# Two tiles at a time in the second half of MoE1, GpSimd subtractions in three slots, and gathers between index loads

## Chip, core and metric

One core of one Trainium2 chip runs the kernel. The metric is the device time of one execution in microseconds (us), as the median of several runs. Engines: TensorE (PE), VectorE (DVE), ScalarE (ACT), GpSimd (POOL) and SyncE (SP, which only issues DMAs).

## What is computed

```python
attn = pooled_attention(q, k, v)        # 8 batches x 8 heads x 576 x 64, k and v mean-pooled by 8
x = attn.transpose(0, 2, 1, 3).reshape(4608, 512)
x = (np.maximum(x @ w_in, 0) ** 2) @ w_out             # MoE1: 512 -> 2048 -> 512
logits = x @ w_gate                                    # MoE2: 8 experts, 512 -> 1024 -> 512
e = argmax(logits, axis=1); p = softmax(logits)[range(4608), e]
out[mask_e] = p[mask_e, None] * (np.maximum(x[mask_e] @ w1[e], 0) @ w2[e])
```

## The kernel before

Everything is fp32 carried through TensorE as pairs: a value is split into a high part (the value rounded to fp32r) and a low part (the rest, rounded), and each product is the sum of three, high·high, high·low and low·high. Tokens go in 18 tiles of 256 (NT); d_ff goes in chunks of 128.

**First half of MoE1** (chunks 0 to 7; names h_a, y_a) runs beside the attention. Each tile's split x is written to DRAM (xs_d), and so is its partial y (yp_d). **Second half** (chunks 8 to 15; names h_b, y_b) is 144 steps, 18 tiles by 8 chunks. A step is layer 1 of a chunk (`layer1`, L291: 12 matmuls of 256 columns into one PSUM tile h), the activation (`act_square_b`, L322 to L325: relu and two squares on ACT, the subtraction gl_b on DVE), some work from a queue, and layer 2 (`layer2`, L342: 6 matmuls of 512 columns) of the chunk two steps back (LAG). `load_xb` brings a tile's xh and xl back from xs_d.

**Routing.** After a tile's last chunk `route` adds the first half's y (L1017, DVE) and puts 16 logits (L1021, DVE: product and sum, written as junk and lg) and a chain of further steps into a queue: rank (L1040 to L1053, DVE), count (L1059, PE, tile pc), place (L1070 to L1087, DVE), two scatters of the positions to perm_d (L1092, POOL, the second waits for the landing of the first) and the store of y to y_d (L1097, POOL). `run_queue` is called twice in a step; the numbers of `many` say how many entries each call runs. After tile 13 (TA) a table of experts is made (table A), then `gather_index` loads each slot's index column (L1244, POOL, pidx) and `gather_rows` gathers its token rows by indirect DMA (L1251, POOL, xg).

**MoE2** (names h_s, y_s) goes in 17 slots of up to 256 tokens of one expert, 8 chunks each, with the same step. A chunk's weights are loaded six items ahead (raw_s, SP) and split three ahead: high part on ACT (L194, wh_s), low part on DVE (L195, wl_s). `slot_xT` transposes gathered rows on PE (L1266, px) and splits them (xh_s on ACT, xl_s on DVE, L610). `act_relu` (L331, L332) makes gh on ACT by a relu of h, and gl on DVE from h and gh; h comes free when both have read it. `moe2_finish` scales y (ACT for the first half of a slot, DVE, L1291, for the second) and scatters both to the output (L1292, POOL). From slot 6 on, half-filled slots are mixed in (hh, hy, hs). Each engine works its instructions off in the order in which the program issues them; the step functions, the queue and two tables of functions by step (`pre`, `post`) set that order:

```python
many = (2, 1) if g < N1 else (1, g % 2)
side = [lambda: run_queue(many[0])]
...
run_queue(many[1])
```

Of the kernel before, what the change touches and what calls it, by code (L numbers as in the profile page):

```python
# [45 lines left out]
def moe_pipeline_kernel(  # L46
# [236 lines left out]
    def layer1(w, x, nm):  # L283
        wh, wl = w
        xh, xl = x
        h = ps_h.tile([P, 256], F32, tag="h", name=f"h_{nm}")
# [6 lines left out]
        return h  # L293

    def act_square(h, nm):
        r = gpool.tile([P, 256], F32, tag="r", bufs=2, name=f"r_{nm}")
        g = gpool.tile([P, 256], F32, tag="g", bufs=2, name=f"g_{nm}")
        gh = gpool.tile([P, 256], F32R, tag="gh", name=f"gh_{nm}")
        gl = gpool.tile([P, 256], F32R, tag="gl", name=f"gl_{nm}")
# [85 lines left out]
    stream = Stream()  # L385

# [966 lines left out]
    def half_step(j, w, first=0, end=NHALF_MOST):  # L1353
        wh, wl = w
        if j < end * NCH:
# [8 lines left out]
            if kk == NK - 1:  # L1364
                hs = halves["pool"].tile([P, 512], F32, tag="hs", name=f"hs_{t}_{half}")
# [12 lines left out]
        if j >= first * NCH + HLAG:  # L1378
# [8 lines left out]
            if c == NCH - 1:  # L1387
                yo = gpool.tile([P, 512], F32, tag="yo", bufs=3, name=f"hyo_{t}")
# [24 lines left out]
    N1 = NT * NCH  # L1413
# [7 lines left out]


# [31 lines left out]
    for i in range(3):  # L1454
        put(pre, i, lambda i=i: wch_b.append(split_raw(fetched[NCH - 3 + i], f"f{NCH - 3 + i}")))
    put(pre, 3, begin_b)
    for ti in range(NT):
        if ti:
            put(pre, (ti - 1) * NCH + 2, lambda ti=ti: xb.update({ti: load_xb(ti)}))
        put(pre, ti * NCH + 4, lambda ti=ti: ypb.update({ti: load_yp(ti)}))  # L1460

    state = None
    for i_, (what, g) in enumerate(items):
# [10 lines left out]
        many = (2, 1) if g < N1 else (1, g % 2)  # L1474
        side = [lambda: run_queue(many[0])]
        if g < N1:
            x = xb[i]
            stream.step(wch_b[c], x, act_square_b, c, state, f"b{i}_{c}",
                        lambda ys, i=i: route(i, ys, ypb[i]), side)
        else:  # L1480
            s = i - NT
# [4 lines left out]
            stream.step(chunks.pop(g - N1), sx[s][0], act_relu, c, state, f"s{s}_{c}", moe2_finish(s), side)  # L1486
# [39 lines left out]
```

## Time and profile before

| | us |
|---|---|
| median of 3 runs (lowest, highest) | 1522.07 (1522.02, 1524.66) |
| the profiled execution | 1524.06 |
| its span, first to last instruction | 1522.5 |
| PE busy in the span | 1461.9 (96%) |
| DVE busy | 1112.9 (73%) |
| ACT busy | 658.2 (43%) |
| POOL busy | 410.2 (27%) |

A group of instructions is told by its line, its engine and what it writes and reads. Times of an instruction run from its start to its end; matmuls overlap, so what one costs is the distance from its start to the start of the next. "Idle before, releaser" says what an engine waited for. The second half of MoE1 runs from about 605 to 1016 us, the slots from there to the end.

### The profile page before, as it was taken

How to read it: one execution, taken by the hardware profiler on the slowest of the kernel's cores; microseconds unless marked ns; L12 is line 12 of the kernel's file. 1: busy time of each engine (PE TensorE's matmuls, PEld its weight loads, DVE VectorE, ACT ScalarE, POOL GpSimd, SP SyncE). 2: the span in 40 equal slices, each digit the busy share in tenths (PEclk: the TensorE clock that was granted, in tenths of full speed). 3: DMA queues.
4: the chain of work that ended last, by engine and by line, in shares of the span. 5: the costliest groups of instructions: out<-in, count | busy, mean ns of one | idle time of the engine just before them, and what ended most of it. 6: DMA issues, size and time to landing. Idle time of an engine off the chain costs nothing. (4 is left out here: it accounts for less than half of the span.)

```text
span 1522.5 us, 26605 instructions
## 1 busy us (share of the span) xinstructions
PE 1461.9 (96%) x9382; PEld 1317.4 (87%) x9382; DVE 1112.9 (73%) x2360; ACT 658.2 (43%) x1376; POOL 410.2 (27%) x507
## 2 busy tenths in 40 slices
PE   5789999999999999999999999999999999999997
PEld 4678889898989999999999999988889888888886
DVE  8986797689867554477777777778785777767763
ACT  4443333233333323433434334345544666655652
POOL 3253334344434444001111111131222222212101
PEclk8799999999999999999999999999999999999998
DMA  9225354456523214765677666578986888888862
GB/s 295 98 88 165 123 155 164 135 174 169 164 87 101 93 61 158 223 97 75 108 98 76 106 97 76 134 158 213 208 253 222 257 258 276 274 254 279 257 223 91
DMA packets 208617, 249.03 MB, mean 164 GB/s; under 512 B 56479, under 2 KB 134431, under 8 KB 208352
## 3 DMA queue, kind: packets, MB, share of 16 engines
q1 hardware_dynamic: 197408, 217.54, 52.1%
q0 software_dynamic: 11072, 29.75, 9.2%
q8 instruction: 75, 1.23, 0.4%
q14 instruction: 62, 0.51, 0.2%
HBM read 193.28 MB, written 55.28 MB: 163 GB/s over the span
## 5 line engine op out<-in xcount | busy, mean ns | idle before, releaser
L1021 DVE CUSTOM_DVE_ANT_0 junk<-yr,wgb 128x512 f32<-128x512 f32 x288 | 198.2, 688 | 4.7
L195 DVE TENSOR_TENSOR wl_s<-raw_s,wh_s 128x1024 fp32r<-128x1024 f32 x136 | 165.6, 1223 | 39.7 <-ACT wh_s L194 38.2
L194 ACT CAST wh_s<-raw_s 128x1024 fp32r<-128x1024 f32 x136 | 141.2, 1046 | 19.7 <-DMA raw_s<-in_moe_w_dram 19.6
L322 ACT ACTIVATE r_b<-h_b 128x256 f32<-128x256 f32 x144 | 55.4, 385 | 213.2 <-PE h_b L291 210.9
L300 ACT ACTIVATE r_a<-h_a 128x256 f32<-128x256 f32 x130 | 50.0, 384 | 212.3 <-PE h_a L291 146.7
L302 POOL TENSOR_TENSOR g_a<-r_a 128x256 f32<-128x256 f32 x130 | 84.3, 649 | 183.7 <-ACT r_a L300 183.2
L1092 POOL DMA_INDIRECT perm_d<-pos,di x36 | 38.7, 1076 | 348.0 <-DVE es L1083 163.2
L325 DVE TENSOR_TENSOR gl_b<-g_b,gh_b 128x256 fp32r<-128x256 f32 x144 | 61.3, 425 | 96.4 <-ACT g_b L324 96.4
L303 POOL TENSOR_TENSOR gl_a<-g_a,gh_a 128x256 fp32r<-128x256 f32 x130 | 97.6, 751 | 102.8 <-DVE gh_a L301 55.2
L342 PE MATMUL y_a<-wh_m,gh_a 128*128 128x512 f32 x288 | 120.4, 418 | 0.0
L342 PE MATMUL y_a<-wh_m,gl_a 128*128 128x512 f32 x288 | 114.8, 399 | 1.0 <-POOL gl_a L314 1.0
L342 PE MATMUL y_a<-wl_m,gh_a 128*128 128x512 f32 x288 | 115.3, 400 | 0.0
L342 PE MATMUL y_b<-wh_f,gh_b 128*128 128x512 f32 x288 | 113.8, 395 | 0.0
L342 PE MATMUL y_b<-wl_f,gh_b 128*128 128x512 f32 x288 | 113.6, 394 | 0.0
L342 PE MATMUL y_b<-wh_f,gl_b 128*128 128x512 f32 x288 | 112.0, 389 | 0.0
L1292 POOL DMA_INDIRECT out_dram<-yo,tidx x34 | 39.5, 1161 | 263.0 <-ACT yo L1289 167.0
L301 DVE SCALAR_TENSOR_TENSOR gh_a<-h_a,r_a 128x256 fp32r<-128x256 f32 x130 | 54.2, 420 | 76.3 <-ACT r_a L300 75.6
L342 PE MATMUL y_s<-wh_s,gh_s 128*128 128x512 f32 x272 | 107.3, 395 | 0.0
L342 PE MATMUL y_s<-wl_s,gh_s 128*128 128x512 f32 x272 | 107.2, 394 | 0.0
L342 PE MATMUL y_s<-wh_s,gl_s 128*128 128x512 f32 x272 | 106.1, 390 | 0.0
L331 ACT ACTIVATE gh_s<-h_s 128x256 fp32r<-128x256 f32 x136 | 52.4, 385 | 114.0 <-PE h_s L291 113.4
L291 PE MATMUL h_a<-xh,wh_m 128*128 128x256 f32 x576 | 98.1, 293 | 2.1 <-ACT r_a L311 1.5
(323 smaller groups left out, 3912.6 us busy)
## 6 DMA issues: line engine op xcount, KB each, us to landing
raw_s<-in_moe_w_dram SPq DMA_DIRECT2D x272, 256.0 KB, 4.2
raw_h<-in_moe_w_dram SPq DMA_DIRECT2D x112, 256.0 KB, 4.0
y_d<-yr POOLq DMA_DIRECT2D x18, 514.0 KB, 10.1
xs_d<-xh SPq DMA_DIRECT2D x18, 512.0 KB, 2.7
xs_d<-xl SPq DMA_DIRECT2D x18, 512.0 KB, 3.3
yp_d<-ya SPq DMA_DIRECT2D x36, 256.0 KB, 2.1
xh_b<-xs_d SPq DMA_DIRECT2D x18, 512.0 KB, 8.5
xl_b<-xs_d SPq DMA_DIRECT2D x18, 512.0 KB, 11.3
```

The lines of the kernel that those rows point to most:

```text
L194: nc.scalar.copy(wh, raw)
L195: nc.vector.tensor_tensor(wl, raw, wh.bitcast(F32), ALU.subtract)
L291: nc.tensor.matmul(h, w_[:, 0, kk * P:(kk + 1) * P], rhs[:, kk, :], start=n == 0, stop=n == 3 * NK - 1)
L300: nc.scalar.activation(r, h, AF.Relu)
L301: nc.vector.scalar_tensor_tensor(gh, h, 0.0, r, op0=ALU.max, op1=ALU.mult)
L302: nc.gpsimd.tensor_tensor(g, r, r, ALU.mult)
L303: nc.gpsimd.tensor_tensor(gl, g, gh.bitcast(F32), ALU.subtract)
L322: nc.scalar.activation(r, h, AF.Relu)
L325: nc.vector.tensor_tensor(gl, g, gh.bitcast(F32), ALU.subtract)
L331: nc.scalar.activation(gh, h, AF.Relu)
L342: nc.tensor.matmul(ys[u], lhs[:, ts], rhs[:, 1, :], start=(c == 0 and n == 0), stop=(c == NCH - 1 and n == 2))
L1021: nc.vector.tensor_tensor_reduce(out=junk, in0=yr[:, u, 0:DM], in1=wgb[:, e, :], scale=1.0, scalar=0.0, op0=ALU.mult, op1=ALU.add, accum_o ...
```

## The change

1. The second half of MoE1 goes in pairs of tiles: `pair_layer1` does a chunk for 512 tokens with 12 matmuls of 512 columns, `pair_act` the activation at that width, layer 2 is unchanged and done for one tile and then for the other, one step back and not two. N1 counts pairs, so there are 72 such steps; `load_pair` brings x in eight DMAs for a pair, in two sets of buffers.
2. In slots 0, 1 and 2 `act_relu_early` makes the relu of h twice on ACT (one fp32r, one fp32), and GpSimd subtracts the one from the other; from slot 3 on `act_relu` stands. The tiles of gh and gl, and those for the scaled y, come from one ring of eight (`ring`).
3. Queue entries in a slot step: (2, 1) in the first eight, (1, 1) up to the 24th, then as before. The table after tile 13 and the first six steps after tile 17 are put in the chain's free places.
4. `after_a` alternates gathers with index loads, and slot 0's rows are transposed in the last two steps of the pairs.

```diff
+    def pair_layer1(w, x, nm):
+        wh, wl = w
+        xh, xl = x
+        h = ps_h.tile([P, 512], F32, tag="h", name=f"h_{nm}")
+        n = 0
+        for w_, x_ in ((wh, xh), (wh, xl), (wl, xh)):
+            for kk in range(NK):
+                nc.tensor.matmul(h, w_[:, 0, kk * P:(kk + 1) * P], x_[kk // 2][:, kk % 2, :], start=n == 0, stop=n == 3 * NK - 1)
+                n += 1
+        return h
...
+    def pair_act(h, nm):
+        r = gpool.tile([P, 512], F32, tag="r", bufs=2, name=f"r_{nm}")
+        g = gpool.tile([P, 512], F32, tag="r", bufs=2, name=f"g_{nm}")
+        gh, gl = ring(f"gh_{nm}"), ring(f"gl_{nm}")
         nc.scalar.activation(r, h, AF.Relu)
         nc.scalar.activation(gh, r, AF.Square)
         nc.scalar.activation(g, r, AF.Square)
...
+    def act_relu_early(h, nm):
+        gh, gl = g_tiles(nm)
+        g = sq_tiles(nm)[0]
+        nc.scalar.activation(gh, h, AF.Relu)
+        nc.scalar.activation(g, h, AF.Relu)
+        nc.gpsimd.tensor_tensor(gl, g, gh.bitcast(F32), ALU.subtract)
         return gh, gl
...
         if ti == TA:
+            fs[10:14] = steps(table_a(), 4)
             fs += after_a()
         if ti == NT - 1:
-            fs += after_b()
+            more = after_b()
+            fs[10:16] = more[:6]
+            fs += more[6:]
...
     def after_a():
-        return (steps(table_a(), 4) + [None] * 2 + [lambda s=s: gather_index(s) for s in range(NSLOT_A)]
-                + [None] * 3 + [lambda s=s: gather_rows(s) for s in range(4)])
+        idx, rows = ([lambda s=s, f=f: f(s) for s in range(NSLOT_A)] for f in (gather_index, gather_rows))
+        return [idx[0], idx[1], None, None, rows[0], idx[2], rows[1], idx[3], rows[2], idx[4], rows[3], idx[5]]
...
-    N1 = NT * NCH
+    N1 = NT // 2 * NCH
...
-        many = (2, 1) if g < N1 else (1, g % 2)
+        many = (2, 1) if g < N1 else (2, 1) if g < N1 + 8 else (1, 1) if g < N1 + 24 else (1, g % 2)
...
-            stream.step(chunks.pop(g - N1), sx[s][0], act_relu, c, state, f"s{s}_{c}", moe2_finish(s), side)
+            stream.step(chunks.pop(g - N1), sx[s][0], act_relu_early if s < 3 else act_relu, c, state, f"s{s}_{c}", moe2_finish(s), side)
```

How the order of instructions moves is shown at three places. PE in the second half of MoE1, before: layer 2 of one chunk and layer 1 of another (x4: four matmuls in a row):

```order
L291 MATMUL h_b_4_8262<-xh_b_7871,wh_f_6926 128x256 x4
L291 MATMUL h_b_4_8262<-xl_b_7872,wh_f_6926 128x256 x4
L291 MATMUL h_b_4_8262<-xh_b_7871,wl_f_6927 128x256 x4
L342 MATMUL y_b_0_0_8244<-wh_f_6860,gh_b_2_8189 128x512
L342 MATMUL y_b_0_0_8244<-wl_f_6861,gh_b_2_8189 128x512
L342 MATMUL y_b_0_0_8244<-wh_f_6860,gl_b_2_8190 128x512
```

and after, where xp are the quarters of a pair's x:

```order
L329 MATMUL h_b_7_6985<-xp_0_6502,wh_f_6751 128x512 x2
L329 MATMUL h_b_7_6985<-xp_0_6505,wh_f_6751 128x512 x2
L329 MATMUL h_b_7_6985<-xp_0_6508,wh_f_6751 128x512 x2
L329 MATMUL h_b_7_6985<-xp_0_6511,wh_f_6751 128x512 x2
L329 MATMUL h_b_7_6985<-xp_0_6502,wl_f_6752 128x512 x2
L329 MATMUL h_b_7_6985<-xp_0_6505,wl_f_6752 128x512 x2
```

Layer 1 of a chunk is 12 matmuls in both; the second serves two tiles.

DVE in slot 0, before (ISA junk: one logit; wl_s: a weight's low part):

```order
L195 TENSOR_TENSOR wl_s_12505<-raw_s_5_12384,wh_s_12504 128x1024
L332 SCALAR_TENSOR_TENSOR gl_s_2_12534<-h_s_2_12520,gh_s_2_12533 128x256
L1021 ISA junk_1_2_12537,lg_12140<-yr_12139,wgb 128x512
L1021 ISA lg_12140 128x1
L195 TENSOR_TENSOR wl_s_12540<-raw_s_6_12438,wh_s_12539 128x1024
L332 SCALAR_TENSOR_TENSOR gl_s_3_12560<-h_s_3_12546,gh_s_3_12559 128x256
```

and after:

```order
L195 TENSOR_TENSOR wl_s_10681<-raw_s_5_10540,wh_s_10680 128x1024
L1081 ISA junk_1_6_10714,lg_10071<-yr_10070,wgb 128x512
L1081 ISA lg_10071 128x1
L1081 ISA junk_1_7_10716,lg_10071<-yr_10070,wgb 128x512
L1081 ISA lg_10071 128x1
L195 TENSOR_TENSOR wl_s_10719<-raw_s_6_10597,wh_s_10718 128x1024
```

The subtraction gl_s is gone from DVE, and the logits of a step are two where one stood.

POOL at the start of the slots, before:

```order
L1251 DMA xg_12179<-y_d,pidx_11986 128x514 x2
L1092 DMA perm_d<-pos_12415,di_12413 37376x1
L1097 DMA y_d<-yr_11768 128x2x514
L1092 DMA perm_d<-pos_12415,di_12413 37376x1
L1292 DMA out_dram<-yo_0_12828,tidx_12264 4608x512
L1292 DMA out_dram<-yo_1_12833,tidx_12264 4608x512
```

and after, where L354 is the subtraction of `act_relu_early` (g_s_0 to g_s_2: chunks 0 to 2 of a slot):

```order
L1314 DMA xg_10502<-y_d,pidx_10421 128x514 x2
L1307 DMA pidx_10527<-perm_d 128x2
L1155 DMA perm_d<-pos_10487,di_10485 37376x1
L1160 DMA y_d<-yr_10058 128x2x514
L354 TENSOR_TENSOR g_s_0_10613<-r_s_0_10614,g_s_0_10613 128x256
L354 TENSOR_TENSOR g_s_1_10670<-r_s_1_10671,g_s_1_10670 128x256
L1155 DMA perm_d<-pos_10487,di_10485 37376x1
L354 TENSOR_TENSOR g_s_2_10709<-r_s_2_10710,g_s_2_10709 128x256
...
L354 TENSOR_TENSOR g_s_1_11012<-r_s_1_11013,g_s_1_11012 128x256
L1355 DMA out_dram<-yo_0_11025,tidx_10507 4608x512
L1355 DMA out_dram<-yo_1_11030,tidx_10507 4608x512
L354 TENSOR_TENSOR g_s_2_11066<-r_s_2_11067,g_s_2_11066 128x256
```

The subtractions of slots 0 to 2 now stand on POOL behind scatters, stores and gathers.

## Rows read from the trace of the kernel before

**Rows 1.** The page: span, and busy time by engine.

```profile
span 1522.5 us, 26605 instructions
PE 1461.9 (96%) x9382; PEld 1317.4 (87%) x9382; DVE 1112.9 (73%) x2360; ACT 658.2 (43%) x1376; POOL 410.2 (27%) x507
```

**Rows 2.** Busy time by stretch: us, then busy and count by engine, clock, DMA share, GB/s.

```profile
605.20:1016.20 411.00, 410.12 (x2681) 372.21 (x2680) 298.45 (x998) 168.69 (x458) 54.71 (x60) 1.00 0.64 109
1016.20:1086.00 69.80, 66.21 (x426) 58.57 (x426) 60.66 (x148) 33.02 (x54) 12.71 (x10) 1.00 0.94 215
```

**Rows 3.** Timeline of PE at its waits, 1006 to 1052: start, us, what, [idle before].

```profile
1006.65 0.63 PE L1266 MATMUL px<-ident,xg 128*128 128x128 f32 x4 [0.88 <-DMA xg<-y_d,pidx]
...
1023.45 0.61 PE L291 MATMUL h_s<-xh_s,wh_s 128*128 128x256 f32 x3 [1.40 <-DVE gl_s L332]
...
1025.53 0.74 PE L291 MATMUL h_s<-xh_s,wh_s 128*128 128x256 f32 x4 [0.40 <-DVE gl_s L332]
...
1043.46 0.74 PE L291 MATMUL h_s<-xh_s,wh_s 128*128 128x256 f32 x4 [1.34 <-DVE gl_s L332]
...
1051.41 0.74 PE L291 MATMUL h_s<-xh_s,wh_s 128*128 128x256 f32 x4 [0.37 <-DVE gl_s L332]
```

**Rows 4.** Timeline of PE in the second half of MoE1, 850 to 858.

```profile
850.83 0.40 PE L342 MATMUL y_b<-wh_f,gh_b 128*128 128x512 f32 x1
...
852.21 0.64 PE L291 MATMUL h_b<-xh_b,wh_f 128*128 128x256 f32 x4
...
853.64 0.40 PE L342 MATMUL y_b<-wh_f,gh_b 128*128 128x512 f32 x1
...
855.03 0.64 PE L291 MATMUL h_b<-xh_b,wh_f 128*128 128x256 f32 x4
...
856.47 0.40 PE L342 MATMUL y_b<-wh_f,gh_b 128*128 128x512 f32 x1
...
857.85 0.64 PE L291 MATMUL h_b<-xh_b,wh_f 128*128 128x256 f32 x4
```

**Rows 5.** A group of DVE's, 1016.2 to 1086: busy us, mean ns | idle before, releaser.

```profile
L195 DVE TENSOR_TENSOR wl_s<-raw_s,wh_s 128x1024 fp32r<-128x1024 f32 x23 | 28.1, 1221 | 8.3 <-ACT wh_s L194 8.3
```

**Rows 6.** Timeline of DVE, 1046 to 1053: what a step's pieces take.

```profile
1046.38 0.68 DVE L1021 CUSTOM_DVE_ANT_0 junk<-yr,wgb 128x512 f32<-128x512 f32 x1
...
1047.11 0.69 DVE L1021 CUSTOM_DVE_ANT_0 junk<-yr,wgb 128x512 f32<-128x512 f32 x1
...
1047.73 1.22 DVE L195 TENSOR_TENSOR wl_s<-raw_s,wh_s 128x1024 fp32r<-128x1024 f32 x1
1048.86 0.41 DVE L332 SCALAR_TENSOR_TENSOR gl_s<-h_s,gh_s 128x256 fp32r<-128x256 f32 x1
...
1051.28 0.16 DVE L1070 TENSOR_TENSOR rk<-pc,base_run 128x16 f32<-128x16 f32 x1
...
1052.72 0.75 DVE L1291 TENSOR_SCALAR yo<-y_s,xg 128x512 f32<-128x512 f32 x1
```

**Rows 7.** DVE and POOL beside each other, 596 to 598.

```profile
596.74 0.74 POOL L303 TENSOR_TENSOR gl_a<-g_a,gh_a 128x256 fp32r<-128x256 f32 x1
596.93 1.62 DVE L195 TENSOR_TENSOR wl_f<-rawf,wh_f 128x1024 fp32r<-128x1024 f32 x1 [0.51 <-ACT wh_f L194]
```

**Rows 8.** Timeline of POOL, 957 to 1085: scatters, and what they waited for.

```profile
957.63 0.96 POOL L1092 DMA_INDIRECT perm_d<-pos,di  x1 [13.12 <-DVE es L1083]
...
965.92 0.99 POOL L1092 DMA_INDIRECT perm_d<-pos,di  x1 [6.59 <-DMA perm_d<-pos,di]
...
1049.91 1.99 POOL L1292 DMA_INDIRECT out_dram<-yo,tidx  x1 [18.25 <-ACT yo L1289]
1056.29 1.87 POOL L1292 DMA_INDIRECT out_dram<-yo,tidx  x1 [4.38 <-DVE lg L1021]
...
1074.28 1.00 POOL L1292 DMA_INDIRECT out_dram<-yo,tidx  x1 [4.93 <-ACT yo L1289]
1084.61 1.33 POOL L1292 DMA_INDIRECT out_dram<-yo,tidx  x1 [9.33 <-issue]
```

More of the change, by code (lines that the diff above doesn't have):

```diff
@@ L285, in layer1 @@
         xh, xl = x
-        h = ps_h.tile([P, 256], F32, tag="h", name=f"h_{nm}")
+        h = ps_h.tile([P, 512], F32, tag="h", name=f"h_{nm}")[:, 0:256]
         n = 0
@@ L293, in layer1, with ring, g_tiles, sq_tiles @@
         return h
+    def ring(nm, dt=F32R):
+        return gpool.tile([P, 512], dt, tag="g", bufs=8, name=nm)
+    def g_tiles(nm):
+        t = ring(f"g_{nm}")
+        return t[:, 0:256], t[:, 256:512]
+    def sq_tiles(nm):
+        t = gpool.tile([P, 512], F32, tag="r", bufs=2, name=f"r_{nm}")
+        return t[:, 0:256], t[:, 256:512]
     def act_square(h, nm):
[L296 to L299, printed above, removed]
+        (r, g), (gh, gl) = sq_tiles(nm), g_tiles(nm)
         nc.scalar.activation(r, h, AF.Relu)
@@ L385, in moe_pipeline_kernel, with __init__, step, pop @@
     stream = Stream()
+    class PairStream:
+        def __init__(self):
+            self.pend = []
+        def step(self, w, x, c, state, nm, finish, between=()):
+            h = pair_layer1(w, x, nm)
+            g = pair_act(h, nm)
+            for f in between:
+                f()
+            self.pend.append((w, g, c, state, nm, finish))
+            while len(self.pend) > 1 + (self.pend[0][2] == 0):
+                self.pop()
+        def pop(self):
+            w, g, c, state, nm, finish = self.pend.pop(0)
+            if c == 0:
+                state["ys"] = [pool.tile([P, 512], F32, tag="y", name=f"y_{nm}_{u}") for pool in (ps_y, ps_y2) for u in range(2)]
+            for i in range(2):
+                us = slice(i * 256, (i + 1) * 256)
+                layer2(w, [t[:, us] for t in g], state["ys"][2 * i:2 * i + 2], c)
+                if c == NCH - 1:
+                    finish(i, state["ys"][2 * i:2 * i + 2])
+                run_queue((1, 2)[i])
     att = ExitStack()
@@ L809, in fin @@
             for u in range(2):
-                yo = gpool.tile([P, 512], F32, tag="yo", bufs=3, name=f"ya_{ti}_{u}")
+                yo = ring(dt=F32, nm=f"ya_{ti}_{u}")
                 if u == 0:
@@ L1260, in slot_xT @@
             nc.vector.tensor_copy(ti_, xg[:, :, DM + 1])
-            sx[s] = new_x(xpool, "x", f"s{s}"), ti_
+            sx[s] = new_x(xpool, "x", f"s{s}") if s else [wraw.tile([P, NK, 256], F32R, tag="raw", name=f"x{i}_s0") for i in range(2)], ti_
         xh, xl = sx[s][0]
@@ L1286, in fin @@
             for u in us:
-                yo = gpool.tile([P, 512], F32, tag="yo", bufs=3, name=f"yo_{s}_{u}")
+                yo = ring(dt=F32, nm=f"yo_{s}_{u}")
                 if u == 0:
@@ L1364, in half_step @@
             if kk == NK - 1:
-                hs = halves["pool"].tile([P, 512], F32, tag="hs", name=f"hs_{t}_{half}")
+                hs = wraw.tile([P, 1024], F32, tag="raw", name=f"hs_{t}_{half}")[:, 0:512]
                 nc.scalar.activation(hs, st["h"], AF.Relu)
@@ L1387, in half_step @@
             if c == NCH - 1:
-                yo = gpool.tile([P, 512], F32, tag="yo", bufs=3, name=f"hyo_{t}")
+                yo = ring(dt=F32, nm=f"hyo_{t}")
                 nc.scalar.activation(yo, st["y"], AF.Copy, scale=st["xg"][:, DM:DM + 1])
@@ L1420, in put, with ahead @@
         d.setdefault(max(g, 0), []).append(f)
+    def ahead(i, n):
+        return i - n if i - n >= N1 else N1 + (i - n - N1) // 2
     H0 = NSLOT_A * NCH + 6
```

70 lines of the change are left out of this document (41 added, 29 removed).

## Prediction

> **What bounds the kernel now.** I read the page first: PE is busy for 1461.9 of 1522.5 us [rows 1]. Then the busy time by stretch: in the second half of MoE1 PE is busy for 410.12 of 411.0 us, and its clock is granted in full (1.00, the 2.4 GHz level) [rows 2]. So there only fewer or shorter matmuls can save time. From 1016 to 1086, the first slots, PE loses 3.6 us, DVE is busy for 60.66 of 69.8, and the DMA engines for 0.94 of it [rows 2]: this is the place where other engines come near PE. Then the timeline at PE's waits: once for the gathered rows (0.88), four times for gl_s on DVE (1.40, 0.40, 1.34, 0.37) [rows 3]. DVE must split weights (wl), make gl and work off the logits of the last tiles, and PE waits for h to be read.
>
> All sums are made against the profiled execution, 1524.06 us, which lies 1.99 above the median of 1522.07; the difference they give is then taken off the median. A measurement of this kernel tells some 0.2% from no change, 3.04 us: below 1519.03 is faster, above 1525.11 slower.
>
> **Pairs in the second half of MoE1.** Layer 1 of a chunk is 12 matmuls of 256 columns for each tile; now 12 of 512 for two tiles. Before, layer 1 starts at 852.21 and layer 2 at 853.64: 1.43 us; again 855.03 to 856.47: 1.44 [rows 4]. Layer 2, 6 matmuls of 512 columns, has as many columns (3072), and takes 1.38, 1.39 and 1.38 (850.83 to 852.21, 853.64 to 855.03, 856.47 to 857.85) [rows 4]. At layer 2's pitch a chunk of a tile saves 1.435 − 1.383 = 0.052 us, and 18 × 8 = 144 of them **7.5 us**. Bounds: the starts are given to 0.01 us, so 0.04 to 0.06, 5.8 to 8.6 us, if layer 1's weights behave as layer 2's do; if 512 columns of layer 1 cost just twice 256, nothing is saved. I take 7.5, since [rows 4] shows the same engine, the same width and the same number of columns. The trace shows 1.435 against 1.383 for the same columns. The Trainium skill, "TensorE: Matmul & The Clock Gate", section "Back-to-back issue gap", gives a matmul of N columns N/2.4 ns and a fixed gap of 2.5 ns on top; by that a pair of 256 loses only 2.5 ns against one of 512, an estimate of 864 × 2.5 ns = 2.2 us in place of 7.5.
>
> The other engines stay under PE there: DVE is busy for 298.45 of 411 us before [rows 2], and wider instructions do the same elements. x comes in eight DMAs of 256 KB for a pair; 2.1 MB at 215 GB/s, which these queues moved [rows 2], is 9.8 us, and it is asked for seven steps before its use, for the first pair five steps of some 2.8: nothing. In the first half of MoE1 the ring and the shared r|g tile change which instruction frees a buffer, on POOL, which is busy for 27% of the span [rows 1]: nothing.
>
> **Waits that go.** The five waits sum to 4.39 us [rows 3]. The idle figure counts from the end of the matmul before, and a matmul of 256 columns lasts 0.16 longer than its pitch of 0.12 (1.435/12; four in a row last 0.64, three pitches and 0.28 [rows 4]), so each costs 0.16 more: 4.39 + 0.8 = **5.2 us**. They go since h in slots 0 to 2 is read by ACT alone, and since the gathers start between the index loads and slot 0's x is made two steps earlier. Bounds 0 to 5.2. What is late next is the weight's low part.
>
> **DVE in slots 0 to 2.** PE takes 2.82 us for a step (852.21 to 855.03 [rows 4]). The split of chunk n stands three steps ahead of its use, which is 0.95 us into its step (the third product). In the changed order I count, from the split of chunk 3 (done about 2.2 us into slot 0: a cast and a split) to that of chunk 26: 23 splits of 1.13 to 1.14 (1047.73 to 1048.86 [rows 6]), 26.2; 42 logits, 0.73 before another logit and 0.61 before something else (1046.38, 1047.11, 1047.73 [rows 6]), 27.4; two rank and two place steps at 1.44 (1051.28 to 1052.72 [rows 6]), 5.7; and twelve passes over 512 columns (six x splits, four adds, two scalings) and three small casts at about a logit's time, 7.6. Together 66.9 us, and no gl. It is 66.9 + 2.2 = 69.1 against 26 × 2.82 + 0.95 = 74.3: 5.1 us early. At chunk 10 the same count is 27.2 + 2.2 against 29.15: 0.2 late, since 19 of the logits stand before it.
>
> But each step puts a subtraction on POOL beside it. Where one runs beside a split, the split takes 1.62 us in place of 1.22: POOL's gl_a starts at 596.74 and lasts 0.74, DVE's wl_f starts at 596.93 [rows 7]. So 0.40 is lost of the 0.55 in which both run, 73%; a subtraction that lies wholly beside a busy DVE takes 0.73 × 0.74 = 0.54. 23 of them: 12.4, and chunk 26 comes 12.4 − 5.1 = **7.3 us late**, which PE waits for piece by piece. Bounds: no loss gives 0.2 (chunk 10), a loss of all 0.74 gives 17.0 − 5.1 = 11.9. I take 0.54, as the row is the nearest there is. DVE idles 8.3 us before wl there, behind ACT's casts [rows 5]; a DVE that is late finds the casts done, so I add nothing (bound: 8.3 more).
>
> **POOL's queue.** Before, no one waits at PE for POOL in the slots; now layer 2 waits for gl, which stands behind scatters. At a slot's end gl of chunk 2 stands behind two output scatters, of which the second starts 6.4 us after the first (1049.91, 1056.29) or 10.3 (1074.28, 1084.61) [rows 8]. Layer 2 comes two steps after the activation, so some 5.2 us are free (2 × 2.82 less the relu and the subtraction): 1.2 or 5.1 late. Twice (ends of slots 0 and 1), at the smaller value, as PE itself is late there: **2.4 us**; bounds 0 to 10.2. In slot 0 gl of chunk 2 also stands behind a second position scatter, which starts 8.3 us after the first (957.63, 965.92 [rows 8]), with two steps between them in the order: 0, and at most 8.3.
>
> **Sum.** −7.5 − 5.2 + 7.3 + 2.4 = −3.0 us: 1521.1 for the profiled execution, **1519.0 us** for the median. By itself this case spans 1512.4 to 1522.2: pairs at 8.6, 0.40 lost per subtraction (9.2 − 5.1 = 4.1 late) and no boundary wait, to pairs at 5.8, 0.60 lost (8.7 late) and 2.4.
>
> **Rivals.**
>
> *B, POOL costs DVE nothing.* Where both meet, POOL is the one that waits, and it has time: 0.74 of work in 2.82 us. For it: a late gl still has the 5.2 us. Against: [rows 7]. Time: −7.5 − 5.2 + 0.2 = −12.5, 1509.6.
>
> *C, a subtraction stops DVE for its whole length.* DVE's lateness is 11.9, and the boundary waits stay: −7.5 − 5.2 + 11.9 + 2.4 = +1.6, 1523.7. It makes the kernel slower than before where one subtraction costs DVE over 0.67 us (5.1 + 10.3 = 15.4 over 23). For it: DVE's queue is dense, so a blocked instruction is always there. Against: 0.40 of 0.55 [rows 7]. The Trainium skill, "SBUF — State Buffer", section "Who interferes with whom", says that a DVE instruction with two SBUF inputs and a GpSimd instruction that reads SBUF lock each other out for the whole instruction; by that rule the loss is nearer 0.74, and the trace agrees in kind (1.62 against 1.22).
>
> *D, 512 columns run at no better pitch in layer 1.* Pairs then give nothing, the lower bound: −5.2 + 7.3 + 2.4 = +4.5, 1526.6. For it: the rows compare two layers, not two widths of one; layer 1 may be slow for another reason, its weights or the tile h. Against: [rows 4], the same columns in less time. The Trainium skill's gap (the section above) would leave 2.2 of the gain, which gives an estimate of 1524.4; the trace's pitch speaks against it.
>
> *E, POOL's queue stops PE.* The scatters' landings in the DMA crowd of 0.94 [rows 2] hold gl: 8.3 in slot 0 and 5.1 at each of two slot ends, 18.5, beside which DVE's lateness hides. −7.5 − 5.2 + 18.5 = +5.8, 1527.9. It decides from 12.7 us of such waits. For it: 10.3 between two scatters [rows 8]. Against: the waits before name DVE and one gather [rows 3], and one long landing is not each.
>
> **How the numbers follow.** A (the sum) 0.40, B 0.24, C 0.16, D 0.08, E 0.12. A lies at the edge of what can be told: I give 0.21 of it to faster, 0.18 to the same, 0.01 to slower. B is faster (0.24). C is the same for 0.10 and slower for 0.06, where pairs give 5.8 and a boundary wait 5.1; D is the same for 0.03 and slower for 0.05. E is slower (0.12). Faster 0.45, same 0.31, slower 0.24. The range goes from B, with half a microsecond for the pitch, to D: 1509.0 to 1527.0; outside are E and the edges of B, C and D, some 0.19.
>
> **What would show it.** In the changed profile the first matmul of a pair's layer 1 and that of layer 2 stand 2.77 us apart, not 2.87, and the second half of MoE1 is 7 us shorter. PE's waits for gl_s from DVE are gone in slots 0 to 2, and the new ones name wl_s from DVE, and gl_s from POOL right behind the output scatters. wl_s has records of 1.6 us and more where a subtraction runs. I am wrong if wl_s stays at 1.22 there (B), if PE waits for POOL over 10 us (E), or if the first half of MoE1 ends more than 2 us away from where it did.

## The result, and the profile after

The change makes the kernel slower: 1537.34 us in the median of six runs against 1523.37 for the kernel before in the same session, a ratio of 1.0093 (95% interval 1.0074 to 1.0113). The prediction, 1519.0 with a range up to 1527.0, is wrong. The profiled execution of the change took 1536.51 us; its page, against [rows 1]:

```profile
span 1534.9 us, 24685 instructions
PE 1457.9 (95%) x8518; PEld 1277.2 (83%) x8518; DVE 1106.7 (72%) x2264; ACT 631.4 (41%) x1184; POOL 435.6 (28%) x531
PEclk7899999999999999999999999999899999999998
```

PE has less work and ends later, and in the 29th slice the granted clock shows an 8. The waits of PE from 600 us on (us in total, times, longest):

```profile
PE y_s L364 <- POOL g_s L354: 15.6, 3, 7.8
PE px L1329 <- DMA xg<-y_d,pidx: 3.1, 1, 3.1
PE h_s L291 <- DVE g_s L346: 2.4, 2, 1.7
```

The waits for gl on VectorE in slots 0 to 2 [rows 3] are gone, as forecast; three waits for POOL are new. The kernel has four stretches. The second half of MoE1 took 411.0 us before [rows 2], and after, from the first row here (us, then busy time by engine, clock, DMA share, GB/s):

```profile
605.10:1008.30 403.20, 400.00 (x1813) 325.77 (x1812) 280.80 (x885) 138.14 (x243) 54.28 (x56) 1.00 0.57 111
...
1026.00:1032.00 6.00, 6.00 (x27) 5.33 (x28) 5.83 (x15) 3.72 (x8) 1.32 (x2) 0.55 0.97 95
...
1056.00:1062.00 6.00, 5.81 (x22) 5.23 (x23) 3.12 (x7) 2.31 (x6) 2.55 (x4) 0.50 0.71 227
...
1090.50:1096.50 6.00, 5.88 (x22) 5.32 (x23) 2.30 (x4) 2.27 (x5) 2.40 (x4) 0.52 0.14 41
```

It starts at the same time (605.1, 605.2) and is 7.8 us shorter. Slots 0 to 2 are measured from the first relu of slot 0 on ACT to the first of slot 3. In the timeline of ACT before:

```profile
1017.88 0.39 ACT L331 ACTIVATE gh_s<-h_s 128x256 fp32r<-128x256 f32 x1 [0.74 <-PE h_s L291]
...
1093.59 0.38 ACT L331 ACTIVATE gh_s<-h_s 128x256 fp32r<-128x256 f32 x1 [1.44 <-PE h_s L291]
```

and after:

```profile
1010.39 0.38 ACT L352 ACTIVATE g_s<-h_s 128x256 fp32r<-128x256 f32 x1 [1.83 <-PE h_s L291]
...
1105.57 0.38 ACT L345 ACTIVATE g_s<-h_s 128x256 fp32r<-128x256 f32 x1
```

75.7 us became 95.2. Slots 3 and 4, by the same marks, took 49.1 and 49.8, and slots 5 to 16, up to their last relu, 364.5 in both. The first relu of slot 0 comes 7.5 us sooner, and what is left behind the last relu is 0.3 shorter. So −7.5 + 19.5 + 0.7 − 0.3 = +12.4, which is what the spans differ by: nearly all that was lost, was lost in slots 0 to 2.

The timeline of POOL there shows how (L354 is the subtraction, L1155 a position scatter, L1355 an output scatter):

```profile
1014.24 1.01 POOL L1155 DMA_INDIRECT perm_d<-pos,di  x1 [4.35 <-DVE yr L1077]
1015.25 0.75 POOL L1160 DMA_DIRECT2D y_d<-yr  x1
1016.02 1.90 POOL L354 TENSOR_TENSOR g_s<-r_s,g_s 128x256 fp32r<-128x256 f32 x2
1023.88 1.17 POOL L1155 DMA_INDIRECT perm_d<-pos,di  x1 [5.96 <-DMA perm_d<-pos,di]
1025.09 1.51 POOL L354 TENSOR_TENSOR g_s<-r_s,g_s 128x256 fp32r<-128x256 f32 x2
...
1045.60 1.29 POOL L1355 DMA_INDIRECT out_dram<-yo,tidx  x1 [0.15 <-issue]
1054.02 1.35 POOL L1355 DMA_INDIRECT out_dram<-yo,tidx  x1 [7.13 <-DVE wl_s L195]
1055.36 1.45 POOL L354 TENSOR_TENSOR g_s<-r_s,g_s 128x256 fp32r<-128x256 f32 x2
...
1077.49 1.82 POOL L1355 DMA_INDIRECT out_dram<-yo,tidx  x1 [0.16 <-ACT r_s L353]
1088.81 0.99 POOL L1355 DMA_INDIRECT out_dram<-yo,tidx  x1 [9.50 <-DMA out_dram<-yo,tidx]
1089.79 2.12 POOL L354 TENSOR_TENSOR g_s<-r_s,g_s 128x256 fp32r<-128x256 f32 x3
```

Each of the three second scatters starts 9.6, 8.4 and 11.3 us after the first, and the subtractions of the next two or three chunks run only behind it. The profile names a landing as what the first and the third of them waited for. For the middle one (1054.02) it names a weight's split on VectorE, but the y that this scatter sends had been ready since 1049.14, so there too the landing of the scatter before it is the likelier cause:

```profile
1048.40 0.74 DVE L1354 TENSOR_SCALAR yo<-y_s,xg 128x512 f32<-128x512 f32 x1
```

At those places PE's timeline has:

```profile
1025.96 0.80 PE L364 MATMUL y_s<-wh_s,g_s 128*128 128x512 f32 x1 [3.90 <-POOL g_s L354]
...
1056.19 0.79 PE L364 MATMUL y_s<-wh_s,g_s 128*128 128x512 f32 x1 [3.85 <-POOL g_s L354]
...
1090.62 0.80 PE L364 MATMUL y_s<-wh_s,g_s 128*128 128x512 f32 x1 [7.82 <-POOL g_s L354]
```

The matmul behind a stop lasts 0.80 us, not 0.39: in the 6 us behind each, the granted clock is 0.55, 0.50 and 0.52 of full (the windows above), near the 1.2 GHz level, so about half of the 18 us is lost: 6 × (0.45 + 0.50 + 0.48) = 8.6 us. Slots 0 to 2 as a whole, before and after (us, then busy time by engine, PE first, clock, DMA share, GB/s):

```profile
1017.88:1093.59 75.71, 72.00 (x467) 63.88 (x466) 66.43 (x161) 36.22 (x58) 17.28 (x13) 1.00 0.95 224
1010.39:1105.57 95.18, 79.61 (x469) 71.10 (x468) 76.84 (x166) 43.30 (x84) 41.22 (x39) 0.87 0.78 166
```

PE is idle for 15.6 us where it was for 3.7, and busy for 79.6 where it was for 72.0, with as many matmuls: 11.9 more of stops and 7.6 more of work, most of what the slow clock's 8.6 would give, are the 19.5.

### The profile page after: what moved, and what is told of

Its sections match the earlier page's. It is cut to its first block, busy times and chain, and to the rows that moved or that the text cites. A ratio compares the mean times of both kernels' runs of the same rounds, so it can differ in the third digit from the quotient of the medians.

```text
span 1534.9 us, 24685 instructions
## 1 busy us (share of the span) xinstructions
PE 1457.9 (95%) x8518; PEld 1277.2 (83%) x8518; DVE 1106.7 (72%) x2264; ACT 631.4 (41%) x1184; POOL 435.6 (28%) x531
## 5 line engine op out<-in xcount | busy, mean ns | idle before, releaser
L364 PE MATMUL y_a<-wh_m,g_a 128*128 128x512 f32 x576 | 208.8, 408 | 1.2 <-POOL g_a L319 1.1
L364 PE MATMUL y_s<-wh_s,g_s 128*128 128x512 f32 x544 | 191.9, 399 | 15.6 <-POOL g_s L354 15.6
L329 PE MATMUL h_b<-xp,wh_f 128*128 128x512 f32 x576 | 144.9, 394 | 0.0
L310 POOL TENSOR_TENSOR r_a<-r_a 128x256 f32<-128x256 f32 x130 | 84.0, 646 | 186.3 <-ACT r_a L308 185.8
L1155 POOL DMA_INDIRECT perm_d<-pos,di x36 | 39.5, 1096 | 342.3 <-DMA perm_d<-pos,di 109.9
L364 PEld LDWEIGHTS y_s<-wh_s,g_s 128*128 128x128 f32 x544 | 104.0, 192 | 35.5 <-POOL g_s L354 16.9
L364 PEld LDWEIGHTS y_a<-wh_m,g_a 128*128 128x128 f32 x576 | 111.0, 193 | 22.3 <-POOL g_a L319 1.5
L311 POOL TENSOR_TENSOR g_a<-r_a,g_a 128x256 fp32r<-128x256 f32 x130 | 98.9, 761 | 103.3 <-DVE g_a L309 32.8
L329 PEld LDWEIGHTS h_b<-xp,wh_f 128*128 128x128 f32 x576 | 107.4, 188 | 23.1
L340 DVE TENSOR_TENSOR gl_b<-g_b,gh_b 128x512 fp32r<-128x512 f32 x72 | 49.8, 692 | 104.4 <-ACT g_b L339 104.3
L364 PE MATMUL y_a<-wl_m,g_a 128*128 128x512 f32 x288 | 115.3, 400 | 0.0
L364 PE MATMUL y_s<-wl_s,g_s 128*128 128x512 f32 x272 | 108.1, 398 | 0.0
L1355 POOL DMA_INDIRECT out_dram<-yo,tidx x34 | 39.5, 1163 | 234.3 <-ACT yo L1352 135.6
```

The source lines that it names most:

```text
L329: nc.tensor.matmul(h, w_[:, 0, kk * P:(kk + 1) * P], x_[kk // 2][:, kk % 2, :], start=n == 0, stop=n == 3 * NK - 1)
L340: nc.vector.tensor_tensor(gl, g, gh.bitcast(F32), ALU.subtract)
L364: nc.tensor.matmul(ys[u], lhs[:, ts], rhs[:, 1, :], start=(c == 0 and n == 0), stop=(c == NCH - 1 and n == 2))
L1155: nc.gpsimd.indirect_dma_start(out=perm_d[:, :], out_offset=bass.IndirectOffsetOnAxis(ap=st["di"][:, u:u + 1], axis=0), in_=st["pos"][:, u ...
```

## The experiments

Sixteen kernels were run. The kernel before was timed beside them in each of four sessions, with medians of 1526.93, 1522.93, 1525.72 and 1526.14 us, so runs are compared by their ratio to it. "Slots 0 to 2" is measured as above.

**Low parts back on VectorE (e1).**

```diff
-            stream.step(chunks.pop(g - N1), sx[s][0], act_relu_early if s < 3 else act_relu, c, state, f"s{s}_{c}", moe2_finish(s), side)
+            stream.step(chunks.pop(g - N1), sx[s][0], act_relu, c, state, f"s{s}_{c}", moe2_finish(s), side)
```

> The change with the low parts of slots 0 to 2 back on VectorE, read from h in PSUM as before the change (no second relu, nothing on GpSimd). Theory P (POOL's queue): the three stops of PE, 15.6 us in all, came from the subtractions standing on GpSimd behind scatters that wait for a landing, and some 8 us more from TensorE's clock at its lower level after each. Without them PE waits nowhere for POOL, the clock row shows 1.00 in the slots, slots 0 to 2 take 76 to 84 us and not 95.2, and the kernel takes 1516 to 1526 us. Rival V (VectorE's queue): the stretch is long because the logits now come closer together; slots 0 to 2 stay above 90 us, PE waits for gl of VectorE instead, and the time stays above 1532.

Ratio 0.9987 (0.9967 to 1.0007). Slots 0 to 2 take 82.6 us, and PE waits nowhere for POOL in the slots:

```profile
PE h_s L291 <- DVE g_s L346: 7.7, 6, 4.6
PE px L1329 <- DMA xg<-y_d,pidx: 2.9, 1, 2.9
```

So the second relu with its subtraction on GpSimd costs 1.0093 − 0.9987 = 1.06%, some 16 us, all of the loss and more. But 82.6 is still over the 75.7 of before, with a stop of PE of 4.6 us in slot 0 and a clock of 0.50 in the 3 us behind it, which theory P did not expect: with low parts where they were, the stretch gives back what the pairs save. How much of the 7 us is the mark's, a later paragraph says.

**The same part alone, on the kernel before (e8).**

```diff
-            stream.step(chunks.pop(g - N1), sx[s][0], act_relu, c, state, f"s{s}_{c}", moe2_finish(s), side)
+            stream.step(chunks.pop(g - N1), sx[s][0], act_relu_early if s < 3 else act_relu, c, state, f"s{s}_{c}", moe2_finish(s), side)
```

> The kernel before, with one part of the change alone: the second relu on ScalarE and the subtraction on GpSimd in slots 0 to 2. Theories P and Q: the subtraction of chunk 2 waits behind the output scatters at the ends of slots 0 and 1, two or three stops of 4 to 8 us with the clock at its lower level after them; PE's waits for gl of VectorE (5 us) go: 4 to 15 us slower than before. Rival V (only the density of the logits matters): 2 to 5 us faster than before.

Ratio 1.0053 (1.0037 to 1.0068): slower, as expected, without pairs and without other queue rates. Slots 0 to 2 take 81.3 us, and PE's waits for POOL are two, the longest of 5.4 us:

```profile
PE y_s L351 <- POOL gl_s L341: 8.3, 2, 5.4
```

**Scatters moved away from the subtractions (e2, e6).** In e2 the second output scatter of slots 0 and 1 comes five steps later, and the second position scatter of tiles 14 to 16 six calls later; e6 moves the output scatters alone.

```diff
-              lambda: route_store(ti, yr), *[None] * SCATTER_GAP, lambda: route_scatter(1, st)]
+              lambda: route_store(ti, yr), *[None] * (SCATTER_GAP + 6 if TA < ti < NT - 1 else SCATTER_GAP), lambda: route_scatter(1, st)]
...
+                def scatter(u=u, yo=yo):
+                    nc.gpsimd.indirect_dma_start(
...
+                if u == 1 and s < 2:
+                    put(post, N1 + (s + 1) * NCH + 7, scatter)
+                else:
+                    scatter()
```

> The change with the subtractions left on GpSimd, but the second output scatter of slots 0 and 1 issued five steps later and the second position scatter of tiles 14 to 16 six queue calls later, so that what they wait for has landed. Theory P: PE's waits for POOL fall from 15.6 to under 3 us, the clock stays at 1.00, slots 0 to 2 take 74 to 82 us, the kernel 1512 to 1524. Rival V: GpSimd still blocks VectorE (logits of 1.23 in place of 0.68 us), so the weight's low part comes late and PE waits for it as the prediction had it, 7 us or more; above 1524.

> As the run before, but only the two output scatters moved; the position scatters stand as in the change. Theory P: the stop of 3.9 us in slot 0 stays, with its clock loss of some 3 us, the two at the ends of slots 0 and 1 go: 5 to 8 us more than with all scatters moved. Rival V: the same time as with all moved, within 2 us.

e2: 1.0036 (1.0014 to 1.0058), slots 0 to 2 in 84.8; e6: 0.9994 (0.9975 to 1.0013), 85.7. In e6 the wait for POOL in slot 0 stays (4.0 us) and the two at the slots' ends are gone, as theory P had it, and by the ratios that is worth about 1%: the subtractions still stand on GpSimd, so this much of the loss is the queue behind the output scatters. A wait of 4.7 us for ScalarE's relu is new, in slot 3. In e2 all waits for POOL but 2.8 us are gone, yet it is slower than e6, where theory P wanted it 5 to 8 us faster: PE now waits for VectorE, for x (2.4), the counts (2.5) and gl (3.7), and for other things. Nor did its clock stay at 1.00: it falls behind stops of 2.4 to 3.6 us (the last section). The page's row of clocks does not show that, as even 6 us at half the clock lower the mean of a slice of 38 us by only 0.08. Theory P's number for e2 failed. Rival V's time holds, above 1524, but its mechanism does not show: no wait of PE names a weight's low part.

**Second relu, subtraction on VectorE (e3).**

```diff
-        nc.gpsimd.tensor_tensor(gl, g, gh.bitcast(F32), ALU.subtract)
+        nc.vector.tensor_tensor(gl, g, gh.bitcast(F32), ALU.subtract)
```

> The change with the second relu on ScalarE kept, and its subtraction on VectorE in place of GpSimd. Theory P: no wait for POOL, clock 1.00, h free after ScalarE alone, so no wait for h either; VectorE has 0.4 us more work a step but is not blocked for 0.55: 1512 to 1522. Rival V: VectorE is full, and PE waits for its low parts: above 1526.

Ratio 0.9983 (0.9963 to 1.0002), the same as e1: h's early release gives nothing that can be told.

**The last tiles one at a time (e4, e5, e7).** NP pairs, then single tiles through the old step, with four queue entries a step there, the old rate in the slots, and slot 0's rows transposed at the old place; e5 is e4 with the subtractions on GpSimd.

```diff
-    N1 = NT // 2 * NCH
+    NP = 7
+    N1 = (NT - NP) * NCH
...
+        if NP * NCH <= g < N1:
+            ti = NP + i
+            stream.step(wch_b[c], xb[ti], act_square_b, c, state, f"b{ti}_{c}",
+                        lambda ys, ti=ti: route(ti, ys, ypb[ti]), side)
```

> Seven pairs (tiles 0 to 13), then tiles 14 to 17 one at a time as before the change, with two queue entries at each call there (four a step), so that only the last tile's routing is left for the slots; the low parts of slots 0 to 2 on VectorE, the queue in the slots at the rate of before. Theory Q (two things stand behind the loss: subtractions in POOL's queue, and a second tile's routing moved into the slots): seven of nine pairs keep 7.7 of the 10 us that pairs save, slots 0 to 2 take 72 to 78 us, no wait for POOL, 0.3 to 0.8% faster than before. Theory P alone (POOL's queue is all of it, routing costs nothing): no better than the first run of this study, which had VectorE's low parts and all nine pairs, and about as long in slots 0 to 2, some 83 us.

> As the run before, but with the second relu and GpSimd's subtraction in slots 0 to 2. Theory Q: POOL's queue still holds gl behind scatters, two stops at the ends of slots 0 and 1 with a fall of the clock, 8 to 20 us slower than the run before. Rival: with VectorE free of half the logits the scaled y comes earlier and POOL's waits stay hidden; within 3 us of the run before.

> As e4, with eight pairs and only tiles 16 and 17 one at a time: about 12 more queue entries are left when the slots begin. Theory Q: 1.1 us more saved by the pair, slots 0 to 2 two to five us longer, about the same time as e4 or up to 4 us slower. Theory P: as e4, 1 us faster.

e4 (NP = 7): 1.0133 (1.0113 to 1.0152), against what was expected. Its second half of MoE1 takes 414.5 us (first relu to first relu of the slots) where the change has 401.5, with PE waiting 3.0 us for a single tile's x and 2.5 for VectorE's counts, and slots 0 to 2 take 86.7. It showed a wait that no theory had, in the waits of ACT:

```profile
ACT g_s L353 <- DMA out_dram<-yo,tidx: 10.8, 2, 9.0
```

gh, gl and the scaled y share one ring of eight buffers since the change, and a relu waits until the output scatter of the y that was last in its buffer has landed. e5 has 1.0182 (1.0161 to 1.0203), 7.5 us over e4, and waits for POOL of 23.7 us in three: the subtractions do worse on GpSimd there too. e7 (NP = 8): 0.9996 (0.9983 to 1.0009), slots 0 to 2 in 76.7, with 11.4 us of the same wait on ACT. That e7 is 1.4% faster than e4, neither theory had.

**Buffers of their own for the scaled y (e9 to e12).** A ring of six, and two buffers for y, on e7, e1, e3 and e2.

```diff
-                yo = ring(dt=F32, nm=f"yo_{s}_{u}")
+                yo = gpool.tile([P, 512], F32, tag="yo", bufs=2, name=f"yo_{s}_{u}")
```

> The run with eight pairs and two single tiles (e7), with the scaled y in two buffers of its own and a ring of six for gh and gl, in the same memory. Theory R (in the ring of eight, an activation's buffer was last a scaled y, and ScalarE waits until its scatter has landed: 11.4 us in three waits in e7): ScalarE's waits for out_dram go, slots 0 to 2 take 73 to 76 us, 3 to 6 us less than e7, 0.2 to 0.5% faster than before. Rival: VectorE's logits and loads are late anyway; within 2 us of e7.

> The run with all nine pairs and the low parts on VectorE (e1), with the scaled y in buffers of its own. Theory R: its 3.9 us of waits for out_dram on ScalarE go and with them the stop of 4.6 us of PE and the fall of the clock behind it: slots 0 to 2 fall from 82.7 to 75 to 79 us, the kernel 3 to 7 us faster than e1. Rival: within 2 us of e1, as the routing of two tiles fills VectorE.

> The run with the second relu and VectorE's subtraction (e3), with the scaled y in buffers of its own. Theory R: h is free after ScalarE and no buffer waits for a scatter; slots 0 to 2 fall from 89.5 to below 84 us. Rival: the second relu gives nothing, since VectorE's subtraction is in the same queue; PE's waits for low parts on VectorE stay above 6 us, and it is no faster than the run before.

> The run with GpSimd's subtractions and all scatters moved (e2), with the scaled y in buffers of its own. Theory R: the 6.0 us in which ScalarE waited for a scatter go; 4 to 8 us faster than e2, about as before the change. Rival V (GpSimd blocks VectorE by 0.55 us at each of 24 subtractions): PE still waits more than 8 us for work of VectorE in slots 0 to 3, and the time stays above that of e10.

e9 0.9983 (0.9961 to 1.0006), e10 0.9983 (0.9962 to 1.0004), e11 0.9983 (0.9965 to 1.0000), e12 1.0055 (1.0033 to 1.0077). ACT's wait is gone in all. Slots 0 to 2 fell from 82.6 to 79.7 in e10 and from 89.5 to 79.5 in e11, but the times hardly moved: e1's and e3's differ from these by less than the intervals. So theory R's numbers failed for e10, whose stop of 4.6 us stays with no wait for a scatter left, and for e9 and e12 too. In e9 the wait came back on VectorE, since two buffers are too few where a scatter is late:

```profile
DVE yo L1368 <- DMA out_dram<-yo,tidx: 8.8, 1, 8.8
```

Its slots 0 to 2 rose from 76.7 in e7 to 83.0. e12 has the same wait (8.7), so it does not tell what it was meant to.

**Four buffers for the scaled y (e13 to e16).** The two of e9 for the first half of a slot, and for the second the two of the squares, which stand idle in the slots; with the ring of six again; on e7, e2, e7 with the second relu on ScalarE, and e1.

```diff
-                yo = ring(dt=F32, nm=f"yo_{s}_{u}")
+                yo = gpool.tile([P, 512], F32, tag="r" if u else "yo", bufs=2, name=f"yo_{s}_{u}")
```

> Eight pairs and two single tiles, low parts on VectorE, ring of six for gh and gl, and four buffers for the scaled y of the slots (two of its own, and the two of the squares, which stand idle there). Theory R (buffers that wait for a scatter's landing give the pairs' gain back): VectorE's wait of 8.8 us for out_dram goes, slot 2 takes 24 to 26 us and not 33.2, the clock stays at 1.00, and the kernel takes 0.3 to 0.7% less than before. Rival: the waits move to low parts that are late for another reason; within 0.2% of before.

> GpSimd's subtractions with all scatters moved, as e12, but with four buffers for the scaled y. Theory V (GpSimd's subtraction takes 0.55 us from VectorE each time, in a stretch where VectorE is full): PE still waits 8 us or more for VectorE's work in slots 0 to 3, slots 0 to 2 take over 82 us, the kernel is 0.2 to 0.5% slower than before and slower than e16 by 6 us or more. Theory P (only the queue): within 3 us of e16.

> As e13, with the second relu on ScalarE and the subtraction on VectorE in slots 0 to 2. If h's release is what PE waits for there, its 3 to 6 us of waits for gl of VectorE go and it is 1 to 5 us faster than e13; if VectorE's queue is what counts, the same time within 2 us.

> All nine pairs, low parts on VectorE (e10), with four buffers for the scaled y. In e10 VectorE and ScalarE waited for no scatter, so theory R expects no change from e10 (1523.0, ratio 0.998) beyond 2 us; slots 0 to 2 stay near 80 us, 4 over before, as two tiles' logits are left for them.

e13: **0.9955 (0.9935 to 0.9975)**, 1518.93 against 1526.14, faster than both kernels. Slots 0 to 2 take 73.8 us, less than before, and the waits of PE from 1000 to 1160 are

```profile
PE h_s L291 <- DVE g_s L354: 4.2, 6, 1.0
PE h_s L291 <- issue: 0.3, 1, 0.3
```

e15 is the same, 0.9957 (0.9939 to 0.9975). e16: 0.9982 (0.9966 to 0.9997), slots 0 to 2 in 80.3. e14, the GpSimd subtractions with no stop by POOL left: 1.0028 (1.0009 to 1.0047), slots 0 to 2 in 85.9; 0.46% or 7 us over e16. Its VectorE from 1008 to 1095, by line (busy us, mean ns):

```profile
L1081 DVE CUSTOM_DVE_ANT_0 junk<-yr,wgb 128x512 f32<-128x512 f32 x46 | 36.9, 802 | 0.5
L195 DVE TENSOR_TENSOR wl_s<-raw_s,wh_s 128x1024 fp32r<-128x1024 f32 x23 | 32.8, 1425 | 5.0 <-ACT wh_s L194 5.0
```

and that of e16:

```profile
L195 DVE TENSOR_TENSOR wl_s<-raw_s,wh_s 128x1024 fp32r<-128x1024 f32 x27 | 32.9, 1219 | 1.8 <-ACT wh_s L194 1.8
L1081 DVE CUSTOM_DVE_ANT_0 junk<-yr,wgb 128x512 f32<-128x512 f32 x46 | 31.5, 685 | 0.6
```

46 logits are 117 ns longer each and 23 splits 206 ns: 5.4 + 4.7 = 10.1 us, or 0.42 for each of 24 subtractions. So GpSimd's work costs twice: by the queue it stands in, and by what it takes from VectorE. That the latter makes all of the 7 us is not shown: e14 and e16 also differ by the second relu and the moved scatters, and of e14's waits some name VectorE (2.5 for the counts, 2.4 for x), one group ScalarE's second relu (2.6).

**The mark of "slots 0 to 2".** It stands on ScalarE, and where ScalarE is late at slot 3, PE is already further on than the mark says. In e1 PE begins slot 3 at 1092.11, and the relu that ends the stretch comes 5 us later, behind a buffer that waits for a scatter:

```profile
1092.11 0.39 PE L291 MATMUL h_s<-xh_s,wh_s 128*128 128x256 f32 x1 [0.20 <-DVE g_s L346]
1097.26 0.39 ACT L345 ACTIVATE g_s<-h_s 128x256 fp32r<-128x256 f32 x1 [0.91 <-DMA out_dram<-yo,tidx]
```

By PE's own marks, from its first matmul of layer 1 in a slot, the falls from e1 to e10 and from e3 to e11 are smaller, and e6 is well ahead of e2, as the times say:

| us | slots 0 to 2, by the relu | by PE's first matmuls | slot 3, by PE |
|---|---|---|---|
| before | 75.7 | 75.7 | 23.4 |
| the change | 95.2 | 95.3 | 23.8 |
| e1 | 82.6 | 79.6 | 24.8 |
| e2 | 84.8 | 83.2 | 31.9 |
| e6 | 85.7 | 77.6 | 31.4 |
| e3 | 89.5 | 82.9 | 29.9 |
| e10 | 79.7 | 78.6 | 24.0 |
| e11 | 79.5 | 78.3 | 24.1 |
| e7 | 76.7 | 76.6 | 23.6 |
| e13 | 73.8 | 75.0 | 23.6 |
| e14 | 85.9 | 84.6 | 25.1 |
| e16 | 80.3 | 78.6 | 24.0 |

Each row is one execution; e3's was its slowest of ten, 6.2 us above its median.

## Why the prediction was wrong, step by step

**Pairs: right in kind, too small.** Forecast 7.5 us. The stretch is 7.8 shorter, though PE waits 3.1 in it for the gathered rows where it waited 0.9 before; without these waits and 0.16 for each the difference is 410.0 − 400.0 = 10.0. In the timeline of PE after:

```profile
848.80 2.03 PE L329 MATMUL h_b<-xp,wh_f 128*128 128x512 f32 x8
...
851.60 0.39 PE L364 MATMUL y_b<-wh_f,gh_b 128*128 128x512 f32 x1
...
854.34 2.03 PE L329 MATMUL h_b<-xp,wh_f 128*128 128x512 f32 x8
```

Layer 1 of a chunk for two tiles takes 2.80 us (2 × 1.435 before), layer 2 of both 2.74 (2 × 1.383 [rows 4]): 0.10 a chunk, 7.2 over 72, some 0.03 of the 0.10 from layer 2, which the sum did not count. The other 2.8 us are not located. Rival D is out. So is the estimate of 2.2 us that the prediction made from the Trainium skill's page "TensorE: Matmul & The Clock Gate", section "Back-to-back issue gap"; the page gives its formula for an isolated matmul and not for a stream. In this stream two matmuls of 256 take 2 × 1.435/12 = 0.239 us and one of 512 takes 2.80/12 = 0.233, 6 ns less, and the measurement decides.

**Waits that go: four of five.** gl on VectorE no longer stops PE in slots 0 to 2: 3.5 us [rows 3], by the sum's way of counting 4.2 of its 5.2. The gather's wait did not go: 0.9 became 3.1. The first gather starts at 996.9 where it started at 1000.7, 3.8 us earlier, but the transposes were moved further ahead than that; a gather earlier still was not tried.

**VectorE in slots 0 to 2: slowed, but not as a wait for wl.** The sum had 7.3 us in which PE waits for the weight's low part. No wait for wl shows in the profile of the change; that VectorE caught up while POOL stopped PE is likely, and not shown. It is slower there by line, from 1008 to 1106:

```profile
L1081 DVE CUSTOM_DVE_ANT_0 junk<-yr,wgb 128x512 f32<-128x512 f32 x46 | 35.2, 766 | 0.6
L195 DVE TENSOR_TENSOR wl_s<-raw_s,wh_s 128x1024 fp32r<-128x1024 f32 x25 | 31.9, 1284 | 0.0
```

Against e16's 685 and 1219 ns that is 3.7 + 1.6 = 5.3 us. The mechanism is visible, POOL's subtraction beside a logit, in the timeline after:

```profile
1038.56 0.83 POOL L354 TENSOR_TENSOR g_s<-r_s,g_s 128x256 fp32r<-128x256 f32 x1 [2.08 <-ACT r_s L353]
1038.71 1.23 DVE L1081 CUSTOM_DVE_ANT_0 junk<-yr,wgb 128x512 f32<-128x512 f32 x1
```

A logit of 0.68 takes 1.23: 0.55 lost, where the sum had 0.54 for a full overlap. Over 24 of them e14 shows 0.42 on the mean, and 6.0 us more in slots 0 to 2 than e16 by PE's marks. That this comes near the forecast of 7.3 is in part luck, as no wait of e14 names wl either. Rival B (nothing lost) is out, and on the mean so is the price of C (all 0.74); single records lose more, the longest split of e14 lasts 2.80 where 1.22 is usual. The lock that the Trainium skill describes ("SBUF — State Buffer", section "Who interferes with whom") agrees in kind: the logit and the split have two inputs in SBUF.

**POOL's queue: the step that failed.** The sum had 2.4 us: 1.2 at each of two slot ends, "as PE itself is late there", and 0 in slot 0. Measured: 3.85, 7.82 and 3.90, 15.6 in all. Three readings were wrong. The second output scatter was taken to come 6.4 us behind the first, the smaller of two rows, and came 8.4 and 11.3. In slot 0 the second position scatter was taken to be covered by two steps, but the first one itself went late: at 1014.24, 6 us into slot 0, after 4.35 us of waiting for VectorE. And PE had lost no time to VectorE by then, which was to cover for POOL. The sum has a slip besides: 5.2 us were said to be free, "2 × 2.82 less the relu and the subtraction", but 5.64 less a relu of 0.39 is 5.25, and the subtraction's 0.74 leaves 4.5. With that and the gaps as measured the same way of counting gives 8.4 − 4.5 = 3.9 and 11.3 − 4.5 = 6.8, against stops of 3.85 and 7.82: the way was right, what was put into it was not. This is rival E's mechanism, which the prediction gave a chance of 0.12, and the sign that it named for E, over 10 us of waits for POOL, is there. E's 18.5 us come near 15.6, but its parts do not: it had 8.3 in slot 0 and 5.1 at each slot's end.

**The clock: a term that was missing.** No case priced what happens behind a stop: 8.6 us at the lower level. With it rival E would have given 1522.07 − 7.5 − 5.2 + 18.5 + 8.6 = 1536.5; that this is near 1537.34 is in part luck, as the kernel before stood at 1523.37 beside the change and E's parts were not those measured.

**What the sum did not ask at all.** e1 has no subtraction on GpSimd, and only breaks even, though its pairs save as much. Tiles 16 and 17 now finish together at the start of the slots, so VectorE has another tile's routing there, and the ring ties relus to scatters. With nine pairs it is the routing that shows: e10 and e16 have no such wait on ScalarE, take the same time as e1, and keep its stop of 4.6 us. In e16 the relu of chunk 1 starts at 1014.16, but its gl stands on VectorE behind four adds of the last pair's y, six logits and a split:

```profile
1013.48 1.28 DVE L1077 TENSOR_TENSOR yr<-y_b,yp 128x512 f32<-128x512 f32 x2
...
1015.29 1.28 DVE L1077 TENSOR_TENSOR yr<-y_b,yp 128x512 f32<-128x512 f32 x2
...
1019.70 0.42 DVE L346 SCALAR_TENSOR_TENSOR g_s<-h_s,g_s 128x256 fp32r<-128x256 f32 x1
```

```profile
1020.17 2.08 PE L291 MATMUL h_s<-x_s,wh_s 128*128 128x256 f32 x8 [4.62 <-DVE g_s L346]
```

e13, which takes the last two tiles singly and gives the scaled y buffers of its own, keeps the gain and has no stop over 1.0 us there. Between e7 and e13 only the buffers differ; between e16 and e13 the last two tiles, with the queue's rate and the place of slot 0's transposes. That each alone is worth its difference to the last microsecond is not shown, as the profiles of one kernel in two executions differ by a few.

## What to carry to other kernels

An engine that is idle most of the time is not free: before work on the path is put into its queue, list what stands ahead of it there and what that waits for, and take the longest such wait seen, not the shortest. Price a stop of TensorE of a few microseconds with the slow clock that may follow it. When a tile moves into a ring with others, ask which DMA must land before its buffer comes round again.

## What the runs showed of the hardware that was not expected

After stops of 3.85, 3.90 and 7.82 us TensorE ran for some 6 us at about half its clock; after the stop of 3.08 us for the gathered rows, and after those of up to 1.40 before the change [rows 3], the windows show 1.00. The length of a stop does not decide it alone: the same wait for the gathered rows, 3.62 us in e2 and 3.63 in e3, was followed by 3 us at 0.50 in e2 and by 6 us at 1.00 in e3, and in e14 one of 2.76 by 3 us at 0.50. What else decides is open. The stops and the windows behind them, e2's first:

```profile
1003.98 1.09 PE L1329 MATMUL px<-ident,xg 128*128 128x128 f32 x4 [3.62 <-DMA xg<-y_d,pidx]
1004.00:1007.00 3.00, 3.00 (x10) 2.52 (x11) 1.20 (x3) 1.90 (x3) 2.39 (x4) 0.50 0.56 147
...
1003.21 0.63 PE L1329 MATMUL px<-ident,xg 128*128 128x128 f32 x4 [3.63 <-DMA xg<-y_d,pidx]
1003.20:1009.20 6.00, 5.99 (x31) 5.03 (x32) 3.90 (x6) 4.94 (x8) 5.08 (x6) 1.00 0.65 181
```

The position scatters, 128 rows each, took 8.3 [rows 8] and 9.6 us from one to the next, about as long as output scatters of half a slot (8.4 and 11.3).
